# A linear-attention layer with a feed-forward block on one Trainium2 core: from one batch to two batches per step after the first chunk, and a new order of the whole program

## The chip, the cores and the metric

The kernel runs on one core of one Trainium2 chip. Five engines with instruction queues of their own work side by side: TensorE (PE; its weight loads are listed as PEld), VectorE (DVE), ScalarE (ACT), GpSimd (POOL) and SyncE (SP). Each engine executes its instructions in the order in which the program gives them, and waits at one whose inputs aren't ready. Transfers between the chip's main memory and the on-chip buffer run on 16 DMA engines that all queues share. SP issues loads, stores and transposes, GpSimd issues the loads of the weights, which it converts from float32 to bfloat16. The metric is the device time in microseconds (us) of one execution.

## The reference

For each of 4 batches and 8 heads a 48 x 48 state is carried over 768 tokens; its rows decay by a gate, and the outer product of k and v is added. The outputs of all heads form rows of 384 values, which go through a feed-forward block with a leaky ReLU between its two matrices.

```python
f = 1.0 / (1.0 + np.exp(-f_logit))
for t in range(S):
    state = f[:, :, t, :, None] * state + np.einsum('bhd,bhe->bhde', k[:, :, t], v[:, :, t])
    y[:, :, t] = np.einsum('bhd,bhde->bhe', q[:, :, t], state)
x = y.transpose(0, 2, 1, 3).reshape(B * S, H * D)      # 3072 x 384
h = x @ w_in                                           # 384 x 2048
out = np.maximum(0.01 * h, h) @ w_out                  # 2048 x 384
```

All inputs and the output are float32: q, k, v and f_logit have 4.7 MB each, of 48 values (192 bytes) per token and head; the two weight matrices have 3.1 MB each.

## The kernel before

The 768 tokens are cut into 6 chunks of 128. A unit is one chunk of one batch, so there are 24 of them, numbered chunk by chunk (unit 4 is the first of chunk 1). Per unit, ScalarE takes exp and ln of the gate (`gate_exp`, `gate_ln`, lines 339 and 342), TensorE sums the logs along the tokens with a triangular matrix (`gate_pe`, L348, and the chunk's total in four matmuls, L351), and ScalarE takes the exponentials of the sum with both signs (`decay_em`, `decay_a`). k and q are multiplied with these (`k_scale`, `q_scale`, L370 and L374) and turned so that the 48 values of a head lie along the partitions: by TensorE (`turn_pe`, L383, with copies out of PSUM) for units 4 to 9, by a DMA transpose per two units (`turn2_dma`, L393) from unit 10 on. Scores (`score_pe`, L420) are masked by VectorE (`mask`, L431), and `mix_pe` (L438, L441) adds what the state and the masked scores give. `state_pe` (L449), `state_dve` and `state_pool` carry the state on. The result y is copied out (`y_out`), turned (`x_pe`, L472, or `x2_dma`) and becomes x.

The feed-forward block takes two units at a time: `up` (L482) makes two of 16 blocks of 128 hidden columns per call, six matmuls of 256 columns, so eight calls per pair; ScalarE applies the leaky ReLU (`up_act`, L487). Units 4 and 5 use `up1` (L493) for one unit. `down` (L502) makes a half of a unit's sum over the 16 blocks, eight matmuls of 384 columns; the last unit is done by column halves (`down_cols`, L507). `put` copies the result out of PSUM and `out_dma` stores it.

The first chunk is done for four batches at once by functions whose names begin with `q_`, with four tokens per partition: its loads have runs of 768 bytes. Later chunks are loaded by `load_part` (L169), one transfer of 197 KB per unit and tensor with runs of 192 bytes, into six buffers per tensor. Weights are loaded by `load_w_in` (L185, two halves) and `load_w_out` (L190, four quarters).

Nothing plans the order at run time. A list of some 850 calls at the end of the function is the program order, and each engine's queue is what that list holds for it, in that order. Some calls only place a load behind another: `touch` (L181) makes GpSimd wait for a tensor's arrival. `idle_pe` (L137) issues matmuls on zeros.

```python
def load_part(u, name, src, eng=nc.sync):
    c, b = units[u]
    t = raws[f"{name}_raw"][u % R_RAW]
    eng.dma_start(out=t, in_=src[b, :, c * C:(c + 1) * C, :].rearrange("h t d -> t h d"))
```

Of the kernel before, what the change touches and what calls it, by code (L numbers as in the profile page):

```python
# [15 lines left out]
def kernel(  # L17
# [15 lines left out]
    NCH = S // C  # L33
# [3 lines left out]
    CH = KD // 2  # L37

    units = [(c, b) for c in range(NCH) for b in range(B)]
    NU = len(units)
    NQ = B

    GBUFS = 5
    R_RAW, R_KQS, R_LF, R_EM, R_AEND, R_V, R_KQT, R_WM, R_XN, R_XT = 6, 4, 3, 3, 8, 6, 4, 4, 4, 4
    const = ctx.enter_context(tc.tile_pool(name="const", bufs=1))
    opool = ctx.enter_context(tc.tile_pool(name="opool", bufs=8))
    psum = ctx.enter_context(tc.tile_pool(name="psum", bufs=1, space=bass.MemoryType.PSUM))
    banks = [psum.tile([128, 512], FP32, name=f"ps{i}", tag=f"ps{i}") for i in range(8)]  # L50

    def ring(name, n, shape, dtype):
        return [const.tile(shape, dtype, name=f"{name}{i}", tag=f"{name}{i}") for i in range(n)]

    def bank(i):
        return banks[i][:, :]

    def bank16(i):
        return banks[i][:, :].bitcast(BF16)

    ctx.enter_context(tc.manual_schedule())


    fq = const.tile([128, H, 4, D], FP32, tag="fq")
    kq = const.tile([128, H, 4, D], FP32, tag="kq")
    qq = const.tile([128, H, 4, D], FP32, tag="qq")

    def first_load(eng, name, b, hh=None):
        h = slice(0, H) if hh is None else slice(4 * hh, 4 * hh + 4)
        eng.dma_start(out=fq[32 * b:32 * b + 32, h, :, :].rearrange("p h j d -> p h (j d)"),  # L70
                      in_=f_logit[b, h, 0:C, :].rearrange("h (t j) d -> t h (j d)", j=4))

    def load_all(t, src):
        nc.sync.dma_start(out=t.rearrange("p h j d -> p h (j d)"),  # L74
                          in_=src[:, :, 0:C, :].rearrange("b h (t j) d -> t b h (j d)", j=4))

    first_load(nc.scalar, "f", 2)
    first_load(nc.sync, "f", 0)
    first_load(nc.scalar, "f", 3, 0)
    first_load(nc.sync, "f", 1, 0)  # L80
    first_load(nc.scalar, "f", 3, 1)
    first_load(nc.sync, "f", 1, 1)
    nc.scalar.preload_act_table_set("natural_log_exp_and_others")
    load_all(kq, k)
    load_all(qq, q)

    AEND = ()
    ut = const.tile([128, 128], BF16, tag="ut")
    make_upper_triangular(nc, ut, val=1.0, diag=True)
    us = const.tile([128, 128], BF16, tag="us")  # L90
    make_upper_triangular(nc, us, val=1.0, diag=False)
    ident = const.tile([128, 128], BF16, tag="ident")
    make_identity(nc, ident)
    ones_col = const.tile([128, 1], BF16, tag="ones")
    nc.gpsimd.memset(ones_col, 1.0)

    w_in_b = [const.tile([128, NK, FF // 2], BF16, name=f"w_in{i}", tag=f"w_in{i}") for i in range(2)]
    w_in_p = [t.rearrange("p a (g n i) -> p a g n i", n=128, i=4) for t in w_in_b]
    w_out_b = const.tile([128, NF, KD], BF16, tag="w_out")

    fill = const.tile([128, 512], BF16, tag="fill")
    nc.vector.memset(fill, 0.0)  # L102
    lfq = [const.tile([128, 4, 4, 64], BF16, name=f"lfq{i}", tag=f"lfq{i}") for i in range(2)]
    khq = [const.tile([128, 4, 4, 64], BF16, name=f"khq{i}", tag=f"khq{i}") for i in range(2)]
    qhq = [const.tile([128, 4, 4, 64], BF16, name=f"qhq{i}", tag=f"qhq{i}") for i in range(2)]
    for t in lfq + khq + qhq:
        nc.vector.memset(t[:, :, :, D:64], 0.0)

    lfs = [const.tile([128, H, 64], BF16, name=f"lf{i}", tag=f"lf{i}") for i in range(R_LF)]
    kqp = ring("kqh", R_KQS // 2, [128, 2, 2, H, 64], BF16)  # L110
    kqs = [kqp[i // 2][:, i % 2] for i in range(R_KQS)]
    khs, qhs = [t[:, 0] for t in kqs], [t[:, 1] for t in kqs]
    state_f = [const.tile([128, P2, D], FP32, name=f"sf{b}", tag=f"sf{b}") for b in range(B)]
    state_b = [const.tile([128, P2, 2 * D], BF16, name=f"sb{b}", tag=f"sb{b}") for b in range(B)]


    block = const.tile([128, 2, 32], BF16, tag="block")
    for b in range(B):
        r = slice(32 * b, 32 * b + 32)
        for i, t in enumerate((ut, us)):  # L120
            nc.vector.tensor_copy(out=block[r, i, :], in_=t[r, r])
    steps = const.tile([128, 4, 32, 4], BF16, tag="steps")
    for i in range(4):
        for t, j0, j1 in ((0, i, 4), (1, 0, i)):
            if j1 > j0:
                nc.vector.tensor_copy(out=steps[:, i, :, j0:j1],
                                      in_=block[:, t, :, None].to_broadcast([128, 32, j1 - j0]))
    for t in lfs:
        nc.vector.memset(t[:, :, D:64], 0.0)
    for t in kqs:  # L130
        nc.vector.memset(t[:, :, :, D:64], 0.0)
    for t in state_b:
        nc.vector.memset(t, 0.0)

    def idle_pe(n, bk):
        for _ in range(n):
            nc.tensor.matmul(bank(bk)[:, 0:256], fill[:, 0:128], fill[:, 0:256], start=True, stop=True)  # L137

    V, A, G = nc.vector, nc.scalar, nc.gpsimd

# [12 lines left out]
    for t in a_rows:  # L153
        nc.gpsimd.memset(t[96:128, :, D:64, :], 1.0)
# [1248 lines left out]
```

## Time and profile before

| | before |
|---|---|
| time, median of 3 runs | 180.19 us (180.1 to 181.2) |
| profiled execution, its own time by its span | 180.2 us |
| TensorE busy | 171.4 us (95%), 1919 matmuls |
| ScalarE busy | 124.4 us (69%) |
| VectorE busy | 92.0 us (51%) |
| GpSimd busy | 57.9 us (32%) |
| granted TensorE clock, mean | 0.998 |
| moved by DMA | 31.31 MB in 109398 packets, of which 100800 under 512 bytes |

The profiled execution has 180.2 us from its first to its last instruction, the same as the median of the timed runs. A row of a group gives engine, operation, output and inputs, shapes and count, then busy time, mean ns of one, and the idle time just before them. A row of the timeline gives start and duration in us. Matmuls are pipelined, so the duration of a single one overstates what it costs in a dense block; there the step from one block's start to the next one's counts.

### The profile page before, as it was taken

Reading aid. Unit: us, or ns where it says so; the run is one execution under the profiler, and the core shown is the slowest. Engines: PE = TensorE matmul, PEld = TensorE weight load, DVE = VectorE, ACT = ScalarE, POOL = GpSimd, SP = SyncE. Lnnn points to the kernel's source line nnn. Section 1 sums busy time; section 2 is a strip of 40 time slices with the busy share of each in tenths; the row PEclk is TensorE's granted clock in tenths of the full one; section 3 lists DMA queues with packets and bytes.
Section 4 is the critical chain, followed back from the end, with each engine's and each line's share of the span. In section 5 each row is a group of like instructions: output and inputs, shape, how many; then the busy total and the mean of one; then the engine's idle time right before and its main releaser. Section 6 shows DMA issues by size and latency. Waiting matters only on the chain.

```text
span 180.2 us, 4849 instructions
## 1 busy us (share of the span) xinstructions
PE 171.4 (95%) x1919; PEld 137.8 (76%) x1919; DVE 92.0 (51%) x211; ACT 124.4 (69%) x264; POOL 57.9 (32%) x107
## 2 busy tenths in 40 slices
PE   7689999999999999899999999999999999999992
PEld 5365899677878897597789687789876697798672
DVE  7779860287888735335376186696543266000000
ACT  2779999286887789767488776668795562596331
POOL 7077570023256444700446052634072100000000
PEclk9999999999999999999999999999999999999999
DMA  5999999899997989999699899999999982720112
GB/s 154 312 299 162 197 208 214 156 201 190 155 205 125 215 172 224 165 216 208 147 239 251 181 183 185 209 213 173 203 155 209 224 237 48 60 77 0 44 48 86
DMA packets 109398, 31.31 MB, mean 174 GB/s; under 512 B 100800, under 2 KB 108096, under 8 KB 109376
## 3 DMA queue, kind: packets, MB, share of 16 engines
q1 hardware_dynamic: 107440, 27.47, 79.5%
q0 software_dynamic: 1376, 3.15, 9.5%
q10 hardware_dynamic: 560, 0.39, 0.7%
q8 instruction: 15, 0.25, 0.7%
q14 instruction: 7, 0.06, 0.1%
HBM read 25.17 MB, written 4.72 MB: 166 GB/s over the span
## 4 chain that ended last, share of the span: by engine, by line
PE 58%; SPq 25%; DMA 11%; issue 1%; ACT 1%; DVE 1%; DVEq 0%
SPq L169 24%; PE ps L482 24%; PE ps L502 23%; DMA v_raw<-in_v_dram 6%; DMA f_raw<-in_f_logit_dram 3%; PE ps L420 2%; DMA fq<-in_f_logit_dram 2%; PE ps L441 2%; PE ps L507 1%; PE ps L438 1%; PE ps L348 1%; SPq L74 1%; PE ps L472 1%; PE ps L449 1%; DVE v_b L145 1%
## 5 line engine op out<-in xcount | busy, mean ns | idle before, releaser
L502 PE MATMUL ps<-w_out_b,gT 128*128 128x384 bf16 x368 | 65.9, 326 | 0.0
L487 ACT ACTIVATE gT<-ps 128x512 bf16<-128x512 f32 x88 | 51.5, 602 | 19.1 <-PE ps L482 16.7
L482 PE MATMUL ps<-xT,w_in 128*128 128x256 bf16 x528 | 63.3, 273 | 1.0 <-DVE xT L145 1.0
L482 PEld LDWEIGHTS <-w_in 128*128 128x128 bf16 x528 | 56.4, 114 | 3.0 <-issue 1.2
L502 PEld LDWEIGHTS <-gT 128*128 128x128 bf16 x368 | 34.6, 98 | 19.8
L431 DVE TENSOR_TENSOR wm<-ps,ut 128x512 bf16<-128x512 f32 x40 | 24.9, 683 | 14.5 <-ACT gT L487 4.9
L370 POOL TENSOR_TENSOR kqh<-k_raw,em_t 128x384 bf16<-128x384 f32 x12 | 11.4, 951 | 33.3 <-ACT em_t L355 28.1
L143 ACT COPY osb<-ps 128x384 f32<-128x384 f32 (+1 forms) x22 | 10.2, 465 | 17.0 <-PE ps L502 15.2
L332 POOL CAST sb<-sf 64x192 bf16<-64x192 f32 x40 | 14.5, 363 | 14.9 <-PE ps L438 12.8
L145 DVE CAST v_b<-v_raw 128x384 bf16<-128x384 f32 x14 | 7.1, 505 | 16.0 <-DMA v_raw<-in_v_dram 15.9
L374 DVE TENSOR_TENSOR kqh<-q_raw,a_t 128x384 bf16<-128x384 f32 x13 | 10.0, 770 | 8.0 <-DMA q_raw<-in_q_dram 7.3
L339 ACT ACTIVATE f_raw<-f_raw 128x384 f32<-128x384 f32 x20 | 10.6, 532 | 4.8 <-DMA f_raw<-in_f_logit_dram 4.6
L342 ACT ACTIVATE lf<-f_raw 128x384 bf16<-128x384 f32 x20 | 10.5, 527 | 0.4
L358 ACT ACTIVATE a_t<-ps 128x384 bf16<-128x384 f32 x20 | 9.8, 494 | 1.1 <-PE ps L351 0.9
L145 DVE CAST xn<-ps 128x384 bf16<-128x384 f32 x15 | 8.2, 556 | 4.1 <-PE ps L441 3.4
L355 ACT ACTIVATE em_t<-ps 128x384 bf16<-128x384 f32 x20 | 9.9, 501 | 0.2 <-PE ps L351 0.2
L463 POOL TENSOR_TENSOR sf<-sf,a_end 128x192 f32<-128x192 f32 x16 | 9.5, 592 | 0.4
L145 POOL CAST v_b<-v_raw 128x384 bf16<-128x384 f32 x6 | 3.1, 510 | 19.8 <-DMA v_raw<-in_v_dram 19.8
L137 PE MATMUL ps<-fill 128*128 128x256 bf16 x37 | 7.3, 353 | 1.4 <-DVE fill L102 1.3
L374 POOL TENSOR_TENSOR kqh<-q_raw,a_t 128x384 bf16<-128x384 f32 x7 | 7.0, 1003 | 4.2 <-issue 2.6
L370 DVE TENSOR_TENSOR kqh<-k_raw,em_t 128x384 bf16<-128x384 f32 x8 | 5.9, 752 | 3.7 <-ACT em_t L355 3.7
L441 PE MATMUL ps<-v_b,wm 128*128 128x48 bf16 x160 | 7.2, 183 | 0.0
(89 smaller groups left out, 201.8 us busy)
## 6 DMA issues: line engine op xcount, KB each, us to landing
out_dram<-osb SPq DMA_DIRECT2D x23, 192.0 KB, 3.4
f_raw<-in_f_logit_dram SPq DMA_DIRECT2D x20, 192.0 KB, 4.6
k_raw<-in_k_dram SPq DMA_DIRECT2D x20, 192.0 KB, 4.6
q_raw<-in_q_dram SPq DMA_DIRECT2D x20, 192.0 KB, 4.5
v_raw<-in_v_dram SPq DMA_DIRECT2D x20, 192.0 KB, 4.2
w_in<-in_moe_w_in_dram POOLq DMA_DIRECT2D x2, 768.0 KB, 9.8
w_out_b<-in_moe_w_out_dram POOLq DMA_DIRECT2D x4, 384.0 KB, 8.4
kq<-in_k_dram SPq DMA_DIRECT2D x1, 768.0 KB, 6.6
```

The source lines that it names most:

```text
L145: eng.tensor_copy(out=out, in_=in_)
L169: eng.dma_start(out=t, in_=src[b, :, c * C:(c + 1) * C, :].rearrange("h t d -> t h d"))
L332: nc.gpsimd.tensor_copy(out=state_b[b][r, :, e * D:(e + 1) * D], in_=state_f[b][r])
L339: nc.scalar.activation(raw[u]["f"], raw[u]["f"], AF.Exp, scale=-1.0)
L342: nc.scalar.activation(lfs[u % R_LF][:, :, 0:D], raw[u]["f"], AF.Ln, bias=1.0)
L370: eng.tensor_mul(khs[u % R_KQS][:, :, 0:D], raw[u]["k"], em_ts[u % R_EM])
L374: eng.tensor_mul(qhs[u % R_KQS][:, :, 0:D], r["q"], a_ts[u % R_EM])
L431: nc.vector.tensor_mul(wms[e][u % R_WM], bank(bk).rearrange("p (i n) -> p i n", i=P2), ut[:, None, :].to_broadcast([128, P2, 128]))
L441: nc.tensor.matmul(bank(bk)[:, h * D:(h + 1) * D], wms[h % 2][u % R_WM][:, h // 2, :], v_b[:, h, :], start=False, stop=(h == H - 1))
L482: nc.tensor.matmul(bank(bk)[:, i * 256:(i + 1) * 256].rearrange("p (a n) -> p a n", a=2), w_in_p[ff // 8][:, kk, ff // 4 % 2, :, ff % 4], ...
L487: nc.scalar.activation(gTs[m % GBUFS][:, 2 * g:2 * g + 2].rearrange("p f a n -> p (f a n)"), bank(bk), AF.Prelu, alpha=0.01)
L502: nc.tensor.matmul(bank(bk)[:, 0:KD], g_part(u)[:, ff, :], w_out_b[:, ff, :], start=(ff == 0), stop=(ff == NF - 1))
```

## The change

The first chunk is now done by batch pairs: loads, gate, turns, scores and x of batches 0 and 1 first, then those of 2 and 3. From chunk 1 on, a step takes a pair of batches, with 64 partitions for each and two tokens per partition, so that runs of a load have 384 bytes; a pair's tensor is loaded by two transfers of 64 partitions. Pairs are numbered as before (pair 2 is units 4 and 5). The logs of a partition's two tokens are added (`gate_sum`), one matmul with a strict triangular matrix per pair sums them (`gate_pe`), and VectorE and GpSimd add the sums back to both tokens (`gate_base`, `gate_next`). `turn_dma` turns k and q of each pair but pair 2 with two DMA transposes of 64 partitions. `v_cast` converts v for the state; `v_spread` copies it with VectorE into the layout of the mix, four copies per pair. `state_pe` takes the two tokens in two half-height matmuls. x goes by `x_pe` for some pairs and `x_dma` for five. All `up` calls take pairs. `w_in` is loaded in four quarters. The order of all calls is new.

```diff
-    def load_part(u, name, src, eng=nc.sync):
-        c, b = units[u]
-        t = raws[f"{name}_raw"][u % R_RAW]
-        eng.dma_start(out=t, in_=src[b, :, c * C:(c + 1) * C, :].rearrange("h t d -> t h d"))
+    def load(n, m, s):
+        c, b = m // 2, m % 2 * 2
+        src = {"F": f_logit, "K": k, "Q": q, "V": v}[n]
+        for w in range(2):
+            nc.sync.dma_start(out=part(n, s)[64 * w:64 * w + 64].rearrange("p h j d -> p h (j d)"),
+                              in_=src[b + w, :, c * C:(c + 1) * C, :].rearrange("h (t j) d -> t h (j d)", j=2))
...
+    def gate_sum(eng, s, l):
+        eng.tensor_add(LS[:, l, :, 0:D], part("F", s)[:, :, 0, :], part("F", s)[:, :, 1, :])
+
+    def gate_pe(end, l, bk):
+        nc.tensor.matmul(bank(bk)[:, 0:KD], tri, LS[:, l, :, 0:D], start=True, stop=True)
...
+    def gate_base(s, bk):
+        t = part("F", s)[:, :, 0, :]
+        V.tensor_add(t, bank(bk)[:, 0:KD].rearrange("p (h d) -> p h d", h=H), t)
+
+    def gate_next(eng, s):
+        t = part("F", s)
+        eng.tensor_add(t[:, :, 1, :], t[:, :, 0, :], t[:, :, 1, :])
...
+    def v_cast(eng, s, t):
+        move(eng, VQ[:, t, :].rearrange("p (j h d) -> p j h d", j=2, h=H), part("V", s).rearrange("p h j d -> p j h d"))
+
+    def v_spread(t, vb):
+        for w in range(2):
+            for j in range(2):
+                V.tensor_copy(out=VB[64 * j:64 * j + 64, vb, w, :], in_=VQ[64 * w:64 * w + 64, t, j * KD:(j + 1) * KD])
+
+    def turn_dma(kh, t):
+        for w in range(2):
+            nc.sync.dma_start_transpose(out=KT[:, t, 1024 * w:1024 * w + 1024].rearrange("p (k n) -> p k n", n=64),
+                                        in_=KH[64 * w:64 * w + 64, kh, :])
...
     def load_w_in(g):
-        w = FF // 2
-        nc.gpsimd.dma_start(out=w_in_b[g],
-                            in_=moe_w_in.rearrange("(a p) n -> p a n", p=128)[:, :, g * w:(g + 1) * w])
+        G.dma_start(out=WI[g], in_=moe_w_in.rearrange("(a p) n -> p a n", p=128)[:, :, g * 512:(g + 1) * 512])
...
+    def state_pe(kh, t, *bks):
+        for p in range(P2):
+            for j in range(2):
+                for w in range(2):
+                    r = slice(64 * w, 64 * w + 64)
+                    x = 2 * p + j
+                    nc.tensor.matmul(bank(bks[w])[:, p * 96:(p + 1) * 96], KH[r, kh, 128 * x:128 * x + 128],
+                                     VQ[r, t, j * KD + p * 96:j * KD + (p + 1) * 96], start=(j == 0), stop=(j == 1))
...
+    put_state(0, 0)
+    gate_ln(2)
+    up(3, 1, 0)
+    q_mul('k', 1, 1, 7, 1)
+    load('Q', 4, 1)
+    v_cast(G, 2, 2)
...
+    gate_sum(G, 2, 0)
+    load('V', 4, 1)
...
+    up(5, 6, 0)
+    up_act(A, 4, 4, 0)
+    v_spread(2, 2)
+    gate_pe(1, 0, 0)
+    down(1, 0, 4, 7, 0)
```

Three places of the new order matter for the prediction. On GpSimd before, in the first chunk, the casts of k, the wait for q and the loads of the weights stand like this (`khq` and `gT` are k and v of the first chunk, `wm` masked scores):

```order
L145 CAST khq_111<-kq 128x16x48
L181 COPY seen<-qq 128x1
L185 DMA w_in_104<-in_moe_w_in_dram 128x3x1024
L185 DMA w_in_103<-in_moe_w_in_dram 128x3x1024
L145 CAST gT_222<-gT_223 128x768 x2
L300 AFFINE_SELECT wm_213<-wm_213 128x512
L300 AFFINE_SELECT wm_211<-wm_211 128x512
L190 DMA w_out_b<-in_moe_w_out_dram 128x1536
```

There the weights go behind the arrival of the first chunk's q, and the first later load that GpSimd itself works on is that of unit 4's successors. In the changed kernel the same place of GpSimd's queue holds the casts of v and k of the first batch pair (`vq`, `kh`) and then the weights:

```order
L142 CAST vq<-rawV 64x1536
L278 COPY seen<-rawV 64x1
L142 CAST kh<-rawK 64x16x48
L281 DMA w_in_83<-in_moe_w_in_dram 128x3x512
L281 DMA w_in_84<-in_moe_w_in_dram 128x3x512
L281 DMA w_in_85<-in_moe_w_in_dram 128x3x512
L281 DMA w_in_86<-in_moe_w_in_dram 128x3x512
L284 DMA w_out<-in_moe_w_out_dram 128x1536 x2
```

All four quarters of `w_in` and half of `w_out` now go out in one go, behind the arrival of the first pair's v and k. GpSimd's queue goes on in the changed kernel with the second batch pair (casts of 64 partitions), the states of batches 0 and 1 (`sb`), and pair 2:

```order
L142 CAST kh<-rawK 64x16x48
L284 DMA w_out<-in_moe_w_out_dram 128x1536 x2
L223 TENSOR_TENSOR wm<-wm,mask_138 128x512
L142 CAST vq<-rawV 64x1536
L142 CAST kh<-rawQ 64x16x48
L271 CAST sb<-sf 64x4x48 x4
L142 CAST vq<-rawV 128x768
L305 TENSOR_TENSOR ls<-rawF 128x8x48
```

The last two rows are `v_cast` and `gate_sum` of pair 2: the sum that feeds the gate's matmul stands behind the cast of V. On SP's queue of the changed kernel the loads of pair 2 follow those of the first chunk, V last (128 partitions in two transfers each, rows with `8x96`):

```order
L152 DMA rawV<-in_v_dram 64x8x192
L152 DMA rawK<-in_k_dram 64x8x192
L152 DMA rawQ<-in_q_dram 64x8x192
L92 DMA rawF<-in_f_logit_dram 32x8x192 x2
L152 DMA rawK<-in_k_dram 64x8x192
L152 DMA rawQ<-in_q_dram 64x8x192
L152 DMA rawV<-in_v_dram 64x8x192
L295 DMA rawF<-in_f_logit_dram 64x8x96 x2
L295 DMA rawQ<-in_q_dram 64x8x96 x2
L295 DMA rawK<-in_k_dram 64x8x96 x2
L295 DMA rawV<-in_v_dram 64x8x96 x2
```

Before, the first chunk's three whole-chunk loads were followed by f, k, q and v of unit 4 alone, with half of these bytes. On TensorE of the changed kernel the last `up` of pair 0's first six and the gate of pair 2 stand next to each other, and the program's first `down` comes behind:

```order
L424 LDWEIGHTS w_in_85
L424 MATMUL ps<-xT,w_in_85 128x256
L308 LDWEIGHTS tri
L308 MATMUL ps<-ls,tri 128x384
L311 LDWEIGHTS ls
L311 MATMUL ps<-ind,ls 128x2
```

Before, the gate of unit 4 (L348) stood ahead of the first `up`, and those of the units behind it after the first `down` calls; now 36 matmuls of `up` stand ahead of the first pair gate.

More of the change, by code (lines that the diff above doesn't have):

```diff
@@ L97 @@
[L97 to L104, printed above, removed]
@@ new lines @@
+    up(4, 4, 3)
+    mask(0, 5)
+    load('V', 11, 1)
+    state_pool(1, 1, 4)
+    up(5, 7, 3)
+    up_act(A, 4, 4, 4)
+    gate_sum(V, 0, 1)
+    put_state(1, 1)
+    turn_dma(0, 0)
+    mix(6, 1, 0, [5, 4], 0, 6)
+    up_act(A, 3, 3, 4)
+    state_dve(0, 1)
+    gate_pe(1, 1, 2)
+    up(6, 0, 3)
+    put_state(2, 0)
+    up_act(A, 5, 7, 4)
+    v_spread(1, 0)
+    up(7, 4, 3)
+    state_pool(0, 0, 4)
+    up_act(A, 6, 0, 4)
+    down(1, 0, 2, 3, 4)
+    gate_base(0, 2)
+    put_state(0, 1)
+    up_act(A, 7, 4, 4)
@@ new lines @@
+    load('K', 10, 0)
+    decay_end(0, 0)
+    up_act(A, 1, 2, 0)
+    up(3, 5, 0)
+    up_act(A, 2, 6, 0)
+    gate_next(G, 2)
+    turn_dma(1, 1)
+    state_pe(1, 2, 1, 3)
+    gate_exp(1)
+    score(1, 2, 4, 0)
+    state_dve(3, 3)
+    score(0, 2, 2, 6)
+    v_cast(G, 0, 2)
+    down(0, 1, 2, 7, 4)
+    decay_a(2, 0)
+    mask(0, 9)
+    state_pool(3, 1, 5)
+    load('Q', 10, 0)
+    gate_ln(1)
+    mask(4, 8)
+    up(4, 3, 0)
+    state_dve(2, 1)
+    decay_em(2, 1)
+    gate_sum(G, 1, 1)
```

2124 lines of the change are left out of this document (954 added, 1170 removed).

## Prediction

> **What bounds the kernel now.** I read the page's busy shares first, then the chain and the timeline of TensorE, then the transfers.
>
> ```profile
> span 180.2 us, 4849 instructions
> PE 171.4 (95%) x1919; PEld 137.8 (76%) x1919; DVE 92.0 (51%) x211; ACT 124.4 (69%) x264; POOL 57.9 (32%) x107
> ```
> TensorE is busy for 95%. Whether it is dense shows in the chain of waits, which gives its blocks without gaps:
>
> ```profile
> 77.01 5.40 PE ps L482 x48
> 83.24 2.60 PE ps L502 x16
> 59.46 0.45 PE ps L383 x8
> 59.90 0.34 PE ps L472 x6
> 61.15 0.55 PE ps L420 x16
> 106.39 0.34 PE ps L449 x8
> ```
> So one matmul costs 0.1125 us (`up`, 256 columns), 0.1625 (`down`, 384), 0.056 (turns and x), 0.034 (scores, 64 rows), 0.043 (states). 576 `up`-sized and 384 `down`-sized ones alone are 127 us. Now the first `up`, and the last matmuls:
>
> ```profile
> 21.10 2.13 PE L482 MATMUL ps<-xT,w_in 128*128 128x256 bf16 x18
> 175.72 1.33 PE ps L507 x16
> 177.07 0.32 ACT osb L143
> ```
> From the first `up` at 21.1 to the end at 177.05 TensorE takes 156.0 us, nearly all of it dense; a tail of 3.1 us follows. **TensorE binds from 21 us on**, and what counts is its work and whatever makes it wait. The profiled execution's own time is its span, 180.2, and the median of the runs shown is 180.19, so sums made against the one hold for the other.
>
> The transfers are the second limit.
>
> ```profile
> 2.00:12.00 10.00, 7.48 (x111) 5.21 (x109) 7.70 (x36) 6.67 (x13) 3.92 (x7) 1.00 1.05 306
> 14.00:32.00 18.00, 17.70 (x211) 15.10 (x211) 11.05 (x28) 16.45 (x34) 8.98 (x18) 1.00 1.09 196
> 40.00:42.00 2.00, 2.00 (x27) 1.42 (x26) 1.97 (x5) 1.04 (x3) 1.64 (x4) 1.00 1.41 186
> q0 software_dynamic: 1376, 3.15, 9.5%
> ```
> The last two columns are the engines' share and GB/s. The first chunk (3.15 MB in 768-byte runs) moves at 306 GB/s and is in by 2 + 3.15/0.306 = 12.3 us. Loads of 192-byte runs alone reach 186. The weights on GpSimd's queue take 9.5% of the span of all 16 engines, 17.1 us. From 14 to 32 us, 3.53 MB moved (196 x 18), and 3.15 MB is the size of the weights: SP's queue got some 0.4 MB, two of its 197 KB loads. Their landings say the same, by tile, for loads issued before 16 us:
>
> ```profile
> 6.42 2.54 SPq L169 DMA_DIRECT2D f_raw<-in_f_logit_dram  x1
> 9.01 2.21 SPq L169 DMA_DIRECT2D k_raw<-in_k_dram  x1
> 11.26 2.22 SPq L169 DMA_DIRECT2D q_raw<-in_q_dram  x1
> 13.52 1.39 SPq L169 DMA_DIRECT2D v_raw<-in_v_dram  x1
> 14.96 14.09 SPq L169 DMA_DIRECT2D f_raw<-in_f_logit_dram  x1
> DMA to landing us min/median/max: 8.3/14.2/20.2
> DMA to landing us min/median/max: 6.9/6.9/6.9
> DMA to landing us min/median/max: 21.1/21.1/21.1
> DMA to landing us min/median/max: 20.4/20.4/20.4
> ```
> The landing rows are those of f (two loads), k, q and v. Units 4's f and k, issued at 6.4 and 9.0, are in at 14.7 and 15.9; its q at 32.4, its v at 33.9, and f of unit 5, issued at 15.0, at 35.2. **While weights are under way, SP's loads hardly move.** Before, nothing on TensorE needs them: it runs the `up` and `down` of the first four units until 35.
>
> **The change part by part.** *TensorE's work.* The gate is summed once per pair. A single gate and its end costs 0.28 us:
>
> ```profile
> 38.23 0.34 PE L348 MATMUL ps<-lf,ut 128*128 128x384 bf16 x1
> 38.41 0.24 PE L351 MATMUL ps<-ones_col,lf 128*128 128x1 bf16 x4
> 38.51 0.83 PE L482 MATMUL ps<-xT,w_in 128*128 128x256 bf16 x6
> 15.66 2.12 PE L264 MATMUL ps<-gT 128*128 128x384 bf16 x12
> ```
> (by the starts: 0.18 and 0.10). 20 gates and 16 ends become 10 and 8: -2.6 us. Turns on TensorE fall from 48 to 16: -1.8; x from 54 to 42: -0.7. States rise from 64 to 128 half-height matmuls: +1.7 at the 0.034 of the half-height scores, +2.8 at 0.043; I take 1.7, the row of the same height. Picking v (16 of 0.18, 2.8 us) becomes 16 spreads into quarter columns, whose form no row shows: between 0.5 us, at the scores' 0.034, and 2.8. With 1.5 the sum is **-4.7 us** (bounds -2.3 to -5.7). `up`, `down`, scores and mixes stay.
>
> *What is left after the first pair gate.* In the new order `gate_pe` (L308) of pair 2 stands after 36 `up` matmuls. Against the 156.0 us that before has left at its first `up`, what follows that gate lacks 36 x 0.1125 = 4.1, 2.3 of gates, 1.8 of turns and 0.7 of x, and has 1.7 more of states and some 0.8 of the second pair's scores and turns: **149.6 us**, with the stalls before had.
>
> *When that gate runs.* It needs `gate_sum` on GpSimd, and that stands behind `v_cast` of pair 2, the cast of V. GpSimd's earlier rows issue all weights. V of pair 2 is the last of the first 17 transfers on SP's queue: behind chunk 0 come F, Q, K, V, 1.57 MB in 384-byte runs. Their rate isn't shown: between 186 and 306 GB/s, 8.4 to 5.1 us; I take 6.0, nearer to the longer runs. The weights keep their 17.1 us, in other pieces. They start as before: before issued them at 11.9 us, after two waits on loads; now GpSimd has its small set-up, a memset of 3072 columns, the cast of 1536 columns and that of K before it. From the rows
>
> ```profile
> 2.38 1.81 POOL L226 MEMSET gT<- 128x2048 bf16 x1
> 8.91 1.21 POOL L145 CAST khq<-kq 128x768 bf16<-128x768 f32 x1 [4.72 <-DMA kq<-in_k_dram]
> 11.93 1.73 POOL L185 DMA_DIRECT2D w_in<-in_moe_w_in_dram  x2
> ```
> that is about 2.4 + 2 + 0.3 + 2.7 + 2.4 + 0.6 + 1.2 = 11.6 us. Since SP's queue gets next to nothing until the weights are in, V lands when all is through: 12.3 + 17.1 + 6.0 = **35.4 us** (37.8 at the low rate; 19 if SP's queue went first). The same sum for before, 12.3 + 17.1 + 0.98 MB/0.186 = 34.7, meets its 35.2. Then the cast (0.83) and the sum (0.95):
>
> ```profile
> L145 POOL CAST gT<-gT 128x768 bf16<-128x768 f32 x2 | 1.6, 828 | 0.2 <-DMA gT<-in_v_dram 0.2
> L370 POOL TENSOR_TENSOR kqh<-k_raw,em_t 128x384 bf16<-128x384 f32 x12 | 11.4, 951 | 33.3 <-ACT em_t L355 28.1
> ```
> With 0.2 for the hand-over the gate starts at 37.4, and the end is 37.4 + 149.6 + 3.1 = **190.1 us**. Queued behind the waiting gate on TensorE are the first `down`, the second pair's scores, and so its x; nothing else feeds TensorE.
>
> The Trainium skill's page "DMA: Bandwidth & Descriptors" (Anatomy of one DMA) fits a GpSimd-issued DMA as 2.0 us plus its bytes over 436 GB/s. By that the weights would take an estimated 7.2 us instead of 17.1, V would be in at about 26, and the end near 180; the 9.5% of the queue's row speak against it, so I keep the row.
>
> *The start.* Chunk 0 goes by batch pairs, and its first `up` should come a little sooner than 21.1, with half the units ready: I estimate 19 to 21 from ScalarE's steps (four of 0.84, two of 0.65, then the second pair's before the first pair's mix). With the wait above this hides entirely.
>
> ```profile
> L234 ACT ACTIVATE fq<-fq 128x768 f32<-128x768 f32 x2 | 1.7, 836 | 1.9 <-DMA fq<-in_f_logit_dram 1.9
> L250 ACT ACTIVATE gT<-ps 128x512 f32<-128x512 f32 x4 | 2.2, 648 | 0.0
> L431 DVE TENSOR_TENSOR wm<-ps,ut 128x512 bf16<-128x512 f32 x40 | 24.9, 683 | 14.5 <-ACT gT L487 4.9
> kqT<-kqh SPq DMA_TRANSPOSE x7, 5.0
> ```
> *The other engines.* ScalarE does the same columns in half as many instructions and loses a few us. VectorE gains 40 copies for spreading v, 10 `gate_base`, five `gate_next`, against fewer v casts: 92 grows to some 110 us, still under TensorE's total but about level with it (42 us each, by counts times rows like the mask's) between the 8th and the 24th `up`. I cost this at nothing in the forecast, since the wait gives it slack; without that cover it costs 0 to 4 us. *Transposes*: SP issues 18 of 256 KB for k and q where it had 7 of 512 KB, each 5.0 us to landing. In the middle SP has room between its loads; I add nothing, and 0 to 5 us is the bound.
>
> **The rivals.** *1: V is in time, and it is faster.* If the engines served SP's queue at its own pace, V would land at 19 to 24 us, TensorE would reach the gate at about 20 + 4.1 + 1 = 25 and never wait there: 25 + 149.6 + 3.1 = **177.7**. The point from which it decides is a landing before 23. For it: runs twice as long, smaller weight pieces, and f and k of unit 4 did land at 14.7 and 15.9, before the weights ran. Against it: the three landings over 20 us. *2: V in time, VectorE sets the pace* in the early stages, where its sum equals TensorE's: 177.7 + 3 = **181**. *3: the wait comes, and more follows:* after 11 us without a matmul the clock drops, or the 18 transposes hold SP's queue so that later loads come late: **193 to 198**. No idle TensorE of that length is in before's trace. The Trainium skill's page "TensorE: Matmul & The Clock Gate" (Part 1) says that after an idle window of about 3.4 us the array runs at half clock until a busy one: that would add an estimated 1.7 us, 192; no run here shows it yet.
>
> **How the numbers follow.** Forecast (late V, 184 to 193): 0.57. Rival 1 (173 to 178.4): 0.26. Rival 2, or a shorter wait (178.4 to 184): 0.10. Rival 3 (above 193): 0.07. The likeliest is 190; its own range is 185 to 193, from V at 31 to 38. The range that holds 8 in 10 has to reach over rival 1: 176.5 to 194. Within 1%, about what a measurement here can tell, lies 178.4 to 182: 0.08; below it 0.26; above it 0.66.
>
> **What would show it.** In the profile after: GpSimd's `v_cast` of pair 2 waiting for a load of V for over 8 us, landings of 15 us or more for the loads issued between 8 and 14 us, a gap on TensorE before the first L308 at about 25 to 37 us, and 150 us from that gate to the last matmul. It is wrong if V lands before 25, if the weights run later than 12 to 33 us, or if stalls later in the run outweigh this one.

## The result, and the profile after

The changed kernel takes **252.8 us** (251.1 to 253.2, 4 runs), the kernel before 180.1 beside it: 1.402 times as long (95% interval 1.395 to 1.409). The forecast was 190, its range 176.5 to 194. The profiled execution of the changed kernel spans 251.0 us. From here on "after" is the changed kernel.

The page of after opens with the span and the engines' busy time; below stand three rows of its 40 slices (6.3 us each).

```profile
span 251.0 us, 4802 instructions
PE 181.6 (72%) x1879; PEld 138.6 (55%) x1879; DVE 119.0 (47%) x247; ACT 113.9 (45%) x193; POOL 82.2 (33%) x136
...
PE   6599401999969989874569720996999999999000
...
PEclk9559975699979999999589995699899999999855
DMA  7999999999679799638789595637541010111111
```

TensorE went from 95% of its span to 72%. It stands still in slices 6 and 7 (31 to 44 us), stops again and again up to slice 28, and the last three slices hold no matmul at all. Where it stops, the granted clock falls (the 5 to 7 in PEclk); the low clock in slices 2 and 3 is taken up at the end.

Three places of after's timeline (start and duration in us, then what ran; in brackets the idle time ahead and what ended it) carry the forecast's three terms: the arrival of V of pair 2, the first pair gate (L308), and the last matmuls (L438).

```profile
26.80 8.11 SPq L295 DMA_DIRECT2D rawV<-in_v_dram  x2
41.39 0.82 POOL L142 CAST vq<-rawV 128x768 bf16<-128x768 f32 x1 [17.08 <-DMA rawV<-in_v_dram]
42.18 0.98 POOL L305 TENSOR_TENSOR ls<-rawF 128x384 bf16<-128x384 f32 x1
43.21 0.48 PE L308 MATMUL ps<-ls,tri 128*128 128x384 bf16 x1 [13.35 <-POOL ls L305]
229.01 2.80 PE L438 MATMUL ps<-w_out,gT 128*128 128x192 bf16 x32
```

V is in at 41.4, the cast and the sum follow, the gate starts at 43.2, the last matmul ends at 231.8. Against the forecast's sum:

| | gate starts | gate to last matmul | tail | span |
|---|---|---|---|---|
| forecast | 37.4 | 149.6 | 3.1 | 190.1 |
| after | 43.2 | 188.6 | 19.2 | 251.0 |
| difference | +5.8 | +39.0 | +16.1 | +60.9 |

The wait that the forecast was built on came; the two larger differences lie behind it. After's waits (time in all, times, longest) and its busy times by stretch (TensorE, its weight loads, VectorE, ScalarE, GpSimd; granted clock, the DMA engines' share, GB/s) show what TensorE met there:

```profile
POOL vq L142 <- DMA rawV<-in_v_dram: 23.8, 5, 17.1
PE ps L365 <- DMA kT<-kh: 23.7, 8, 10.8
ACT rawF L299 <- DMA rawF<-in_f_logit_dram: 19.6, 5, 10.5
PE ps L308 <- POOL ls L305: 15.8, 3, 13.4
```

```profile
2.00:12.00 10.00, 6.39 (x67) 4.35 (x67) 9.40 (x35) 5.08 (x8) 8.82 (x20) 0.77 1.06 207
0.00:70.00 70.00, 48.05 (x554) 35.45 (x554) 47.00 (x105) 36.70 (x58) 38.03 (x66) 0.83 1.06 205
70.00:232.00 162.00, 133.58 (x1325) 103.16 (x1325) 71.98 (x143) 76.98 (x135) 44.14 (x70) 0.93 0.59 108
232.00:250.00 18.00, 0.00 (x0) 0.00 (x0) 0.00 (x0) 0.17 (x1) 0.00 (x0) 0.62 0.13 47
```

The scores (L365) wait 23.7 us for transposed k and q, the exps for F, GpSimd for V. In the last 18 us nothing runs but stores, at a share of **0.13 of the 16 DMA engines: two of them**, moving 47 GB/s. In the trace's packets, exactly two are under way for 85% of that stretch and three for most of the rest. Before, the first 70 us hold 65.4 us of TensorE and the rest of it is full:

```profile
0.00:70.00 70.00, 65.44 (x826) 52.70 (x827) 46.10 (x124) 54.16 (x118) 29.31 (x55) 1.00 1.05 199
70.00:177.00 107.00, 105.94 (x1097) 85.14 (x1094) 45.87 (x88) 69.92 (x148) 28.56 (x52) 1.00 0.83 159
```

### The profile page after: what moved, and what is told of

It reads as the page before. It is cut to its first block, busy times and chain, and to the rows that moved or that the text cites. A ratio compares the mean times of both kernels' runs of the same rounds, so it can differ in the third digit from the quotient of the medians.

```text
span 251.0 us, 4802 instructions
## 1 busy us (share of the span) xinstructions
PE 181.6 (72%) x1879; PEld 138.6 (55%) x1879; DVE 119.0 (47%) x247; ACT 113.9 (45%) x193; POOL 82.2 (33%) x136
## 4 chain that ended last, share of the span: by engine, by line
PE 34%; DMA 15%; issue 4%; SPq 4%; ACT 4%; POOL 3%; DVE 0%; POOLq 0%; ACTq 0%
PE ps L433 15%; PE ps L424 15%; DMA kT<-kh 8%; DMA rawF<-in_f_logit_dram 4%; SPq L347 4%; POOL kh L335 2%; DMA rawV<-in_v_dram 2%; DMA xT<-xn 1%; PE ps L365 1%; PE ps L438 1%; ACT xn L140 1%; ACT rawF L302 1%; ACT rawF L299 1%; PE ps L386 1%; ACT em L326 1%
## 5 line engine op out<-in xcount | busy, mean ns | idle before, releaser
L424 PE MATMUL ps<-xT,w_in 128*128 128x256 bf16 x576 | 72.7, 282 | 2.1 <-ACT gT L429 2.0
L433 PE MATMUL ps<-w_out,gT 128*128 128x384 bf16 x368 | 69.0, 343 | 0.0
L369 DVE TENSOR_TENSOR wm<-ps,mask 128x512 bf16<-128x512 f32 x40 | 25.6, 685 | 29.1 <-PE ps L365 28.9
L142 DVE COPY osb<-ps 128x384 f32<-128x384 f32 (+1 forms) x11 | 5.9, 539 | 42.7 <-PE ps L433 36.5
L365 PE MATMUL ps<-kT 64*128 64x128 bf16 x160 | 7.9, 236 | 23.7 <-DMA kT<-kh 23.7
L343 DVE COPY vb<-vq 64x384 bf16<-64x384 bf16 x40 | 16.2, 406 | 16.8 <-POOL vq L142 14.9
L365 PEld LDWEIGHTS <-kT 64*128 64x128 bf16 x160 | 5.1, 103 | 27.4 <-DMA kT<-kh 25.6
L271 POOL CAST sb<-sf 64x192 bf16<-64x192 f32 x40 | 14.3, 358 | 12.3 <-DVE sf L264 5.5
L142 POOL CAST vq<-rawV 128x768 bf16<-128x768 f32 (+1 forms) x10 | 10.0, 1003 | 24.0 <-DMA rawV<-in_v_dram 23.8
L299 ACT ACTIVATE rawF<-rawF 128x768 f32<-128x768 f32 x10 | 8.3, 846 | 19.6 <-DMA rawF<-in_f_logit_dram 19.6
L396 POOL TENSOR_TENSOR sf<-sf,aend 128x192 f32<-128x192 f32 x16 | 8.7, 546 | 22.8 <-DVE sf L393 22.3
L308 PE MATMUL ps<-ls,tri 128*128 128x384 bf16 x10 | 3.6, 358 | 15.8 <-POOL ls L305 15.8
L335 POOL TENSOR_TENSOR kh<-rawQ,aa 128x384 bf16<-128x384 f32 x14 | 13.7, 998 | 3.8 <-issue 1.9
L393 DVE TENSOR_TENSOR sf<-sf,ps 64x192 f32<-64x192 f32 x32 | 11.2, 350 | 3.3 <-PE ps L386 2.8
L335 DVE TENSOR_TENSOR kh<-rawK,em 128x384 bf16<-128x384 f32 x12 | 9.4, 819 | 4.1 <-ACT em L326 4.1
```

Source lines behind the costliest of these rows:

```text
L142: eng.tensor_copy(out=out, in_=in_)
L271: G.tensor_copy(out=SB[r, b, s, :, e * D:(e + 1) * D], in_=SF[r, b])
L299: A.activation(RAW["F"][:, s], RAW["F"][:, s], AF.Exp, scale=-1.0)
L335: eng.tensor_mul(o[:, :, j, :, 0:D], x[:, :, j], y[:, :, j])
L343: V.tensor_copy(out=VB[64 * j:64 * j + 64, vb, w, :], in_=VQ[64 * w:64 * w + 64, t, j * KD:(j + 1) * KD])
L365: nc.tensor.matmul(bank(bks[e])[:, p * 128:(p + 1) * 128], turned(t, w, 0, p)[r], turned(t, w, 1, p)[r], start=True, stop=True)
```

## Experiments: the stores

Two tokens now lie on one partition pair 64 apart, so a store writes DRAM rows 2t+j from partition 64j+t, and `out_rows` gives the transfer a leading dimension of 2 (4 in the first chunk). The tail's two engines suggest that this dimension sets how many engines a store uses. The changed kernel with that dimension taken out of the transfer (`a_out16`):

```diff
     def out_dma(u, J, o):
-        nc.sync.dma_start(out=out_rows(u, J), in_=OS[:, o])
+        for j in range(J):
+            r = slice(C // J * j, C // J * (j + 1))
+            nc.sync.dma_start(out=out_rows(u, J)[j], in_=OS[r, o])
```

(`out_cols` likewise.)

> The changed kernel, with each store of a result issued as 2 (first chunk: 4) stores, one per token of a partition, so that no store has a leading dimension of 2 or 4; same bytes, same places. Theory A (a store with a leading dimension of 2 runs on two of the 16 DMA engines and holds up every load and transpose that shares them): the tail behind the last matmul falls from 19 to about 3 us, the waits for kT, rawF and rawV in mid-run (23.7, 19.6 and 23.8 us) fall to under half, 251 becomes 200 to 215. Rival B (the slow stores cost only the tail): about 235, the mid-run waits stay. Rival C (the tail is something else): 251, and more SP issues add 1 to 3 us.

Measured: 224.2 us (222.6 to 224.6), ratio 1.235 (1.225 to 1.244): 28 us less. The tail is 4.2 us, and waits in mid-run fell too. These are waits of `a_out16`:

```profile
PE ps L308 <- POOL ls L305: 15.1, 2, 13.6
PE ps L365 <- DMA kT<-kh: 13.1, 7, 2.6
ACT rawF L299 <- DMA rawF<-in_f_logit_dram: 11.6, 5, 3.7
POOL vq L142 <- DMA rawV<-in_v_dram: 20.9, 5, 16.9
```

The waits for kT and F came down to 55 and 59% and their longest from over 10 us to under 4, so it is more than the tail. Theory A is right in kind, but it asked for under half, the wait for V hardly moved (23.8 to 20.9), and 224 lies above its 200 to 215. The first gate's wait did not change: the first store goes out at 58.7, behind it.

To price the form alone it was put into the kernel before. The first try was an empty one (`b_out2`): with `"(j t) n -> j t n"` the two dimensions follow each other in memory and merge again.

> The kernel before with the DRAM side of each whole store cut as (j t) with j = 2 outermost, as in the changed kernel; rows, bytes and everything else the same. Theory A (two engines carry a store: 4.72 MB of results at the 34 to 50 GB/s of the changed kernel's tail are over 95 us of those two engines, next to the loads that take 79.5% of the span on all): 220 to 255. Rival B (only the tail): 181 to 186. Rival C (the form of a store costs nothing): 180.

Measured: 181.3 us, ratio 1.000 (0.997 to 1.004). It only says that nothing else in such an edit costs time. With `"(t j) n -> j t n"`, as in the changed kernel (`b_tj`; the rows of the result come out permuted):

```diff
-        eng.dma_start(out=out[b * S + c * C:b * S + (c + 1) * C, :], in_=st[u].pop("osb"))
+        eng.dma_start(out=out[b * S + c * C:b * S + (c + 1) * C, :].rearrange("(t j) n -> j t n", j=2), in_=st[u].pop("osb"))
```

> The kernel before with each whole store written to DRAM rows 2t+j from partition 64j+t, so that its DRAM side has a real leading dimension of 2, as in the changed kernel (rows of the result come out permuted; bytes and row length are the same; in the run with (j t) the two dimensions merge into one, so that it tested nothing). Theory A (two engines carry each store and hold up the loads that share them): 200 to 255, waits of DVE and ACT for loads grow, landings of stores grow from 3.4 us. Rival B (only a tail): 181 to 190. Rival C (the form costs nothing): 180.

Measured: **233.9 us, ratio 1.294** (1.286 to 1.301), from one rearrangement of 23 stores with the same bytes. Waits of `b_tj`, then the same four of before:

```profile
DVE v_b L145 <- DMA v_raw<-in_v_dram: 44.9, 9, 14.6
ACT f_raw L339 <- DMA f_raw<-in_f_logit_dram: 34.2, 10, 10.8
POOL v_b L145 <- DMA v_raw<-in_v_dram: 26.7, 4, 11.0
PE ps L348 <- ACT lf L342: 16.9, 5, 8.8
```

```profile
POOL v_b L145 <- DMA v_raw<-in_v_dram: 19.8, 6, 5.2
DVE v_b L145 <- DMA v_raw<-in_v_dram: 15.9, 8, 3.1
ACT f_raw L339 <- DMA f_raw<-in_f_logit_dram: 4.6, 7, 1.1
PE ps L348 <- ACT lf L342: 0.3, 1, 0.3
```

No engine's waits in `b_tj` name a store until the end; the loads behind them are what comes late, F by up to 10.8 us where it was 1.1, and TensorE's gate (L348) with it. Two ways can lead there, and no run separates them. The loads keep all 16 engines busy (a share of 1.05 in before's first 70 us), so each can be held by its part on the two engines that carry the stores; and SP, which issues in order, is held longer at each load (median for k and q from 60 us on 1.4 us, before 0.8). The Trainium skill's page "DMA: Bandwidth & Descriptors" (Rules for kernel authors, "Use all 16 engines") says that the number of engines comes from the slowest dimension that isn't 1, and that an outermost dimension of size c under 16 confines the transfer to at most c engines. The trace agrees: 0.13 of 16 is 2.1 engines, in the tail of after.

## Experiments: the wait for V

The forecast's one cause, tested by moving `v_cast` of pair 2 behind the scaling of that pair and `v_spread` behind its last `turn_out` (`a_order`), alone and with the split stores (`a_out_order`):

```diff
-    v_cast(G, 2, 2)
...
-    v_spread(2, 2)
...
     scale(G, 1, 2, 0, 2)
+    v_cast(G, 2, 2)
...
     turn_out(V, 1, 1, 2)
+    v_spread(2, 2)
```

> The changed kernel with two calls moved: GpSimd's v_cast of pair 2 behind the scaling of k and q of that pair, VectorE's v_spread of pair 2 behind the last turn_out of it. The first pair gate then needs F of pair 2 alone and not V. The theory of the prediction (V's landing sets the gate): TensorE's gap at 27 to 42 us shrinks by 8 to 13 us, and the time falls by as much, to 239 to 244. Rival (the loads and transposes behind the gap are late by themselves, so the gap only moves): 249 to 253.

> Both edits. If the two causes are separate places of the run, the gains add: about 190 to 205. If the stores alone set the pace: as with the stores alone. If it ends under 185, little else of the change costs time; what is left over 180 is the price of transposes, half-partition loads and VectorE.

Measured: 260.1 us (ratio 1.437, 1.427 to 1.447) and 232.1 us (1.279, 1.271 to 1.288): 7 to 8 us slower than without the move, both times. The edit has a flaw: the load of pair 5's V into the same buffer stands ahead of the moved cast, so the cast waits for that later load and works on its data. The timeline of `a_order` shows both halves of the matter all the same:

```profile
31.11 0.52 PE L308 MATMUL ps<-ls,tri 128*128 128x384 bf16 x1
...
55.75 1.59 POOL L142 CAST vq<-rawV 128x768 bf16<-128x768 f32 x2 [16.06 <-DMA rawV<-in_v_dram]
...
56.60 1.65 DVE L343 COPY vb<-vq 64x384 bf16<-64x384 bf16 x4 [14.09 <-POOL vq L142]
58.29 0.36 DVE L142 COPY xT<-ps 128x384 bf16<-128x384 bf16 x1
```

The gate goes at 31.1 instead of 43.2, so **V did hold the first gate, by 12 us**. But the wait moved to VectorE, in front of the copy of x that TensorE needs next.

So pair 2's work was moved whole, with the loads that reuse its buffers, behind the x of batches 2 and 3 (`a_late`; its core, with the lines that left their old places left out), and the same with split stores on ScalarE's queue (`a_lateA`; those of column halves stay on SP's); `a_outA` has those stores alone.

```diff
     up_act(A, 7, 2, 0)
+    q_back_out(A, 2, 4)
+    gate_sum(G, 2, 0)
+    gate_pe(1, 0, 2)
+    up(0, 3, 1)
+    gate_base(2, 2)
+    decay_end(2, 0)
...
+    scale(G, 1, 2, 0, 2)
+    v_cast(G, 2, 2)
+    scale(V, 0, 2, 0, 2)
+    load('F', 5, 2)
...
+    turn_out(V, 1, 1, 2)
+    v_spread(2, 2)
     score(1, 2, 1, 0)
```

> The changed kernel with pair 2's work (gate, scaling, turns, v, and the loads of pair 5 that reuse its buffers) moved on every engine behind the x of batches 2 and 3, and three of the up calls of pair 1 and the end of the first down moved in front of or among it. Nothing else changes. TensorE then has the mixes of pair 1 and some 10 us of up and down to do before it needs pair 2's F. Theory of the prediction (the gate in front of that work costs the gap at 27 to 42 us): 238 to 244. Rival (the loads of later pairs are late by as much, so the gap comes back later): 249 to 253.

> The changed kernel with one store per token of a partition, as in the run that split the stores, and all of these issued by ScalarE's queue instead of SP's. Theory D (what is left after the split is SP's queue: 23% of the chain of waits there is SP issuing, and transposes stand in it behind loads and 58 stores): 224 falls to 205 to 215, the waits for kT shrink, ScalarE's gT loses some. Rival (the loads' rate and buffers set the pace, not SP): 222 to 227.

> Both: pair 2's work late, and split stores on ScalarE's queue. If the places are separate, the gains add: 190 to 205. If they share one cause, the loads' supply: within 3 us of the better one.

Measured: `a_late` 256.7 us (1.417, 1.412 to 1.423), `a_outA` 229.2 (1.261, 1.251 to 1.270), `a_lateA` 231.6 (1.279, 1.272 to 1.285). Late work gains nothing (4 us more than after), and stores on ScalarE's queue are 5 us worse than on SP's: theory D as put there fell.

## Experiments: transposes, loads, the first chunk

What else holds the run was found by leaving things out, all with split stores. `a16_noturn` has no DMA transposes of k and q (`turn_dma` loops over nothing, and the scores use old data), `a16_noload` no loads from pair 5 on (pairs 5 to 11, 7 of 10 pair loads, not the 11 of 14 of the expectation), `a16_q128` one transfer to 128 partitions for each of the first chunk's k, q and v; and `b_half` is before with those three loads cut in two:

```diff
-        nc.sync.dma_start(out=t.rearrange("p h j d -> p h (j d)"),
-                          in_=src[:, :, 0:C, :].rearrange("b h (t j) d -> t b h (j d)", j=4))
+        for r in range(2):
+            nc.sync.dma_start(out=t[64 * r:64 * r + 64].rearrange("p h j d -> p h (j d)"),
+                              in_=src[:, :, 64 * r:64 * r + 64, :].rearrange("b h (t j) d -> t b h (j d)", j=4))
```

> The changed kernel with split stores and without its 18 DMA transposes of k and q (left out: the turning of pairs 3 and on, whose scores then use old data). Theory D (the transposes, 3.2 us of SP's queue each pair and 4 to 6 us to landing, hold TensorE and SP's later loads): 224 falls by 15 to 25 us, to 200 to 209. Rival F (supply by loads and buffers sets the pace): 218 to 224.

> The changed kernel with split stores and without the loads of pairs 5 to 15 (left out: 11 of 14 pair loads of f, k, q and v; old data stand in). Theory F (the loads' supply through three buffers per tensor sets the pace from 55 us on): 224 falls by 15 to 30 us, towards 195 to 205. Rival D (the transposes or the chain of work of one pair): less than 8 us, 216 to 224.

> The changed kernel with split stores, and the first chunk's k, q and v each by one transfer to all 128 partitions as before (the rows of that chunk then lie in another order, so its results differ; the work is the same). Theory E: the first chunk is in some 4 to 5 us sooner, V of pair 2 lands that much sooner, the first pair gate starts at 37 to 38 instead of 42 us, and 224 becomes 218 to 221. Rival (later places set the time, as in the run with pair 2's work late): 222 to 226.

> The kernel before with the first chunk's loads of k, q and v cut into two transfers of 64 partitions each; same bytes and runs. Theory E (a transfer to 64 partitions moves at about two thirds of the rate: the changed kernel's first chunk goes at 210 GB/s where before has 306): GB/s over 2 to 12 us falls from 306 towards 210, k, q and v land up to 5 us later, the time rises by 2 to 5 us, to 182 to 186. Rival (the low rate comes from what else runs then): still about 300 GB/s, 180 to 181.

Measured: `a16_noturn` 203.9 us (1.126, 1.119 to 1.133), 20 less than `a_out16`; `a16_noload` 208.4 (1.148, 1.140 to 1.155), 16 less; `a16_q128` 217.6 in one run, the profiled one, and 221.2 to 221.5 in three, 3 to 7 less; `b_half` 183.1 (1.013, 1.006 to 1.020), 2 more than before. Without the transposes TensorE is dense from 70 us on (stretches of `a16_noturn`):

```profile
0.00:70.00 70.00, 48.00 (x556) 35.83 (x556) 48.22 (x108) 36.67 (x58) 38.00 (x66) 0.83 1.05 208
70.00:197.00 127.00, 125.76 (x1325) 100.27 (x1324) 70.99 (x140) 76.70 (x134) 45.44 (x70) 0.99 0.48 104
```

125.8 of 127 us, where after has 133.6 of 162. The first 70 us are as bad as in after: 48.0, and 17.4 short of before. The cut loads show in the stretch from 2 to 12 us, first `b_half`, then `a16_q128`:

```profile
2.00:12.00 10.00, 6.46 (x66) 4.39 (x64) 6.31 (x32) 5.37 (x8) 3.32 (x5) 0.92 1.06 228
```

```profile
2.00:12.00 10.00, 6.70 (x69) 4.49 (x69) 9.08 (x37) 5.09 (x8) 8.61 (x18) 0.78 1.06 291
```

Before has 306 GB/s there and falls to 228 with the loads in halves; the changed kernel has 207 and rises to 291 with them whole. The engines' share is 1.06 in both: just as busy, with fewer bytes. With the loads whole, V of pair 2 is in at 36.8 and the first gate starts at 38.7, 4.0 us sooner than in `a_out16` (`a16_q128`):

```profile
36.83 0.82 POOL L142 CAST vq<-rawV 128x768 bf16<-128x768 f32 x1 [12.93 <-DMA rawV<-in_v_dram]
...
38.66 0.48 PE L309 MATMUL ps<-ls,tri 128*128 128x384 bf16 x1 [11.57 <-POOL ls L306]
```

The same page of the Trainium skill (Rules for kernel authors) says not to cut a transfer into two partition halves, since both use the same engines. The runs go further than no gain: the rate is 25% lower in halves in the kernel before and 29% in the changed one. The time that this costs is 2 us in the one and 3 to 7 in the other.

Four more runs asked how these causes combine. `a_noturn` is after without the transposes, its stores as they are; `a16_turn2` issues the second transpose of a pair from ScalarE (`(nc.sync, nc.scalar)[w]`); the other two add the late order, and the late order and the whole first loads, to `a16_noturn`.

> The changed kernel, stores as they are, with the DMA transposes of k and q left out. If the stores on few engines cost through the transposes that cross them, the middle of the run is dense and only the tail of 19 us stays above the run without both: 204 + 16 = 220. If they hold up the loads by themselves too: 230 to 240.

> Split stores, and of each pair's two DMA transposes the second issued by ScalarE's queue instead of SP's. If the transposes cost through SP's time (3.2 us for each pair ahead of loads and stores), half of the 20 us that leaving them out gave comes back: 224 falls to 212 to 216. If they cost by their landing (4.3 us) and by what they hold up in the engines: 221 to 227; the wait on ScalarE's own queue for scaled k and q can add to that.

> Split stores, the DMA transposes of k and q left out, and pair 2's work late. With the transposes left out TensorE is dense from 70 us on, so a gap saved ahead of that is no longer taken back. Theory of the prediction (the wait for V costs what the gap lasts, 13.5 us): 204 falls to 189 to 195. Rival (the loads of pairs 3 to 5 are late by themselves, and the gap moves behind the late work): 199 to 205.

> Split stores, no DMA transposes of k and q, pair 2's work late, and the first chunk's k, q and v each by one transfer to 128 partitions. All four causes taken away: if they make up the 72 us, what is left is the kernel of the prediction's faster rival: 177 to 184. If something else costs, over 187.

Measured: `a_noturn` 223.0 us (1.231, 1.225 to 1.237), `a16_turn2` 264.1 (1.459, 1.449 to 1.468), `a16_noturn_late` 207.3 (1.146, 1.138 to 1.155), which is 3 more than `a16_noturn` and above both of its expected ranges, the last 202.7 (1.121, 1.116 to 1.127), far above the 177 to 184 that it should show if these four causes were all. The first gate and the last matmuls of `a_out16`, of `a_noturn` and of `a16_noturn`, in that order, give the same three terms as above:

```profile
42.67 0.48 PE L308 MATMUL ps<-ls,tri 128*128 128x384 bf16 x1 [13.65 <-POOL ls L305]
...
215.75 2.80 PE L438 MATMUL ps<-w_out,gT 128*128 128x192 bf16 x32
```

```profile
43.29 0.48 PE L308 MATMUL ps<-ls,tri 128*128 128x384 bf16 x1 [12.93 <-POOL ls L305]
...
199.64 2.80 PE L438 MATMUL ps<-w_out,gT 128*128 128x192 bf16 x32
```

```profile
42.91 0.48 PE L308 MATMUL ps<-ls,tri 128*128 128x384 bf16 x1 [13.49 <-POOL ls L305]
...
194.28 2.81 PE L438 MATMUL ps<-w_out,gT 128*128 128x192 bf16 x32
```

| stores | DMA transposes | gate starts | gate to last matmul | tail | span |
|---|---|---|---|---|---|
| as changed | yes (after) | 43.2 | 188.6 | 19.2 | 251.0 |
| split | yes | 42.7 | 175.9 | 4.2 | 222.8 |
| as changed | no | 43.3 | 159.2 | 18.9 | 221.3 |
| split | no | 42.9 | 154.2 | 4.3 | 201.4 |

The tail is the stores' alone, 15 us. In the middle the two feed each other: the stores cost 12.7 us beside the transposes and 5.0 without them, the transposes 29.4 beside slow stores and 21.7 beside split ones.

`a16_turn2` did not decide what it was made for. SP's queue in it shows why:

```profile
SPq L347 <- DMA kT<-kh: 34.7, 4, 11.1
SPq L454 <- DMA kT<-kh: 24.2, 3, 13.2
```

A transpose on one queue waited there for the other queue's to land, and SP's stores stood behind that. It shows the price of such waits on SP's queue and nothing on where the 20 us come from. The last two runs asked again. `a16_noturn_late2` is `a16_noturn_late` with the exps of F of pairs 3 and 4 moved behind pair 2's as well; `a16_scratch` lets the transposes write to a buffer that nothing reads.

```diff
-    gate_exp(0)
     x_pe1(1, 1, 0)
     x_pe1(0, 1, 3)
-    gate_exp(1)
...
     up_act(A, 2, 2, 1)
+    gate_exp(0)
+    gate_exp(1)
     down(1, 3, 4, 7, 0)
```

```diff
-            nc.sync.dma_start_transpose(out=KT[:, t, 1024 * w:1024 * w + 1024].rearrange("p (k n) -> p k n", n=64),
+            nc.sync.dma_start_transpose(out=KX[:, t, 1024 * w:1024 * w + 1024].rearrange("p (k n) -> p k n", n=64),
```

> As the run with split stores, no transposes and pair 2's work late, and the exps of F of pairs 3 and 4 moved behind it too: in that run they waited for their loads until 43 and 45 us, with the copy of x for pair 1 behind them on ScalarE, and TensorE idled from 39 to 47. Theory of the prediction (only the order makes TensorE wait for pair 2): TensorE works through 30 to 47 us, and 204 (without the late order) falls to 191 to 197. Rival (the whole supply of pairs 2 to 4 is late, and the gap comes wherever the first pair work stands): 200 to 208.

> Split stores, and the transposes write to a buffer that nothing reads (the scores of pairs 3 and on use old data, and nothing waits for a transpose to land). If their landing costs TensorE the 20 us: 204 to 209, as without them. If their time on SP's queue and their room among the loads cost it: 218 to 224.

Measured: `a16_scratch` 221.6 us (1.231, 1.222 to 1.241), within 3 of `a_out16`. **TensorE's wait for a transpose to land is not what the transposes cost**: with nothing on TensorE waiting for them the run is nearly as long, and the waits are elsewhere (of `a16_scratch`; `a_out16` has no such wait for xT):

```profile
PE ps L425 <- DMA xT<-xn: 7.1, 2, 5.6
ACT rawF L300 <- DMA rawF<-in_f_logit_dram: 14.0, 5, 4.2
```

They cost by what they hold up: SP's queue in order, with the loads of later pairs and the transposes of x behind them, and room in the engines. Which of these two weighs more wasn't separated. That leaving out loads gives 16 us fits either.

`a16_noturn_late2` took 200.8 us (1.113, 1.107 to 1.119), 3 less than `a16_noturn`. TensorE does work where it stood still, and the first 70 us hold 52.9 us of it instead of 48.0:

```profile
39.26 0.34 PE L308 MATMUL ps<-ls,tri 128*128 128x384 bf16 x1
...
0.00:70.00 70.00, 52.91 (x574) 38.63 (x575) 50.96 (x114) 36.64 (x58) 38.50 (x67) 0.84 1.06 210
```

The rest of the 13 us came back as smaller waits up to 70 us: from 43 to 70 us it works 18.8 us there, where `a16_noturn` has 24.8. So the rival of that run holds for most of it (200.8 lies in its 200 to 208): pairs 2 to 4 are late as a whole. No version tried here beats the kernel before.

## Why the prediction was wrong

*The wait for V came as described, and nearly as long; what it was worth was wrong.* The cast of V ahead of `gate_sum` did hold the first gate: GpSimd waited 17.1 us for V, TensorE 13.4, and the gate went 31.1 instead of 43.2 once V was out of its way. That SP's loads hardly move beside the weights held too: F of pair 2, issued at 9.0, was in at 26.1. V came at 41.4 and not at 35.4: of the sum 12.3 + 17.1 + 6.0 the term that was too small is the first one, the first chunk at 306 GB/s. That rate was taken from loads to 128 partitions; in halves the chunk moves at 207, its last load was in at 19.2, and the last of the weights at 38.2 (issued at 16.6, 21.6 us to landing), past the 33 us that the forecast named as a sign of being wrong. With whole loads V came 4.0 us sooner. What the 13 us are worth is less than the forecast made of them: only 3 of them came back in `a16_noturn_late2`.

*"149.6 us, with the stalls before had" failed.* TensorE's work behind the gate was sized well: without stalls from stores and transposes it takes 154.2. Some 3.5 of the 4.6 us between are an estimate of what the clock took: from 42.9 to 46.7 and from 70.6 to 74.0 us of `a16_noturn` TensorE is busy for 7.2 us at a granted 0.52. But 34 us of new stalls came (29 with the transposes beside slow stores, 5 from the stores alone), and the forecast had no term for them. The step that failed is "In the middle SP has room between its loads; I add nothing, and 0 to 5 us is the bound". Leaving the transposes out is worth 20 us beside split stores and 30 beside slow ones. The forecast looked at a transpose's own 5.0 us to landing, and not at what stands behind it in SP's queue, which each pair's work now passes twice; that it is the queue, and not the room in the engines, is argued and not shown.

*The tail of 3.1 us was carried over from before and is 19.2.* This step failed too: the forecast took the stores to cost what they had cost before. The form of the stores was in the diff's reach (`out_rows` gives a leading dimension of the tokens per partition) and no part of the forecast speaks of it. This is the largest single miss: 28 us in after, 53 when put into the kernel before. Why it costs more there wasn't tested.

*Of the rivals*, the third named the transposes on SP's queue and the clock, but stopped at 198. The clock did fall: 0.83 on the mean of the first 70 us. The Trainium skill's page "TensorE: Matmul & The Clock Gate" (Part 1) has the array at half clock after an idle window of about 3.4 us; the trace agrees in kind (0.58 to 0.74 in the stretches with the gap). VectorE came to 119 us, not 110, and TensorE's waits for it are small in after (3.2 us for `kh` the largest): rival 2 didn't arise. Rival 1 needs V before 23 us; the earliest that a run shows is 36.8.

*What stays open.* Without slow stores and without transposes 21 us are left over before's 180.2 (201.4), and the first 70 us of TensorE lack 17.4. The forecast had 9.9 of the 21 itself; against its terms this run has the gate 5.5 later, 4.6 more behind it and 1.2 more in the tail. Order (3 us, `a16_noturn_late2`) and whole first loads (3 to 7 us, and 4.6 from `a16_noturn_late` to 202.7) each gave back little; the better order and whole loads together were not run. That one queue brings the chunk, then pairs 2 to 5, beside the weights, is argued from the timeline, not shown.

## What to carry to other kernels

When a layout changes, look at the access pattern of every transfer that it changes, stores too: a small leading dimension on the DRAM side put whole stores on two DMA engines, and the loads behind them came late. A forecast of one wait has to ask what the same queue holds next; here three causes were worth 28, 20 and 3 us, and the one that was foreseen was the least. Leaving a cause out, alone and in pairs, told more than moving calls about, since every move shifted the wait to the next engine in order.

## What was not expected of the hardware

The granted clock can be low where TensorE is busy: from 10 to 20 us after has 9.4 us of matmuls at a mean clock of 0.61, behind a first stretch with 5.8 us of them. What sets this off isn't shown: before has 6.6 us in the first stretch and a clock of 1.00 behind it, `b_half` 6.5 and 0.66. At 43.6 us after runs at a granted 0.50, at 53.1 at 1.00, and four matmuls of `down` take 1.44 us at the one and 0.81 at the other:

```profile
0.00:10.00 10.00, 5.83 (x48) 3.91 (x48) 8.77 (x37) 4.92 (x6) 8.14 (x25) 0.87 0.87 168
10.00:20.00 10.00, 9.41 (x146) 7.08 (x143) 7.90 (x15) 7.12 (x10) 8.56 (x12) 0.61 1.14 206
...
43.63 1.44 PE L433 MATMUL ps<-w_out,gT 128*128 128x384 bf16 x4
...
53.13 0.81 PE L433 MATMUL ps<-w_out,gT 128*128 128x384 bf16 x4
```

So busy time counts a matmul at half clock as nearly twice as long, and TensorE's 181.6 us in after can't be set against before's 171.4 as work. And two transposes on two queues did not go side by side: SP's queue waited for ScalarE's to land, whether by the chip or by a wait in the program isn't shown, and the run with them was the slowest of all, 264 us.
